# Finer pieces and other places for the weights of an mLSTM cell and a multiplicative FFN on one Trainium2 core

## The chip, the cores and the metric

The kernel runs on one core of a Trainium2 chip. The metric is the device time of one execution in microseconds (us). The core has five engines with a queue each: TensorE (PE, matmuls; its weight loads are listed as PEld), VectorE (DVE), ScalarE (ACT), GpSimd (POOL) and SyncE (SP, which here only issues DMAs). An engine works through its own instructions in order and waits for others by semaphores. Traces are taken by the hardware profiler; times in them are us from the start of the span.

## The reference, cut to what matters

```python
# q, k, v, o_gate: (4, 8, 768, 40); i_gate, f_gate: (4, 8, 768); all float32
for t in range(768):                                   # mLSTM cell
    m_new  = max(f[t] + m, i[t])
    C = exp(f[t] + m - m_new) * C + exp(i[t] - m_new) * outer(v[t], k[t])
    n = exp(f[t] + m - m_new) * n + exp(i[t] - m_new) * k[t]
    y[t] = sigmoid(o_gate[t]) * (C @ q[t]) / max(|n . q[t]|, 1)
    m = m_new
x   = y as (3072, 320)                                 # tokens x (heads * dims)
out = (((x @ w1) * (x @ w2)) @ w3) @ w_out             # w1, w2: 320x1024, w3: 1024x1024, w_out: 1024x320
```

The four weights arrive as 64-bit floats, so that each of their elements is two 32-bit words, and the kernel turns them into 32-bit floats itself.

## The kernel before

**Units and steps.** The cell is computed in chunks. A unit n is 128 tokens of one batch (two chunks of 64, all 8 heads); there are 24 of them (NU), and n = 4c + b. The main loop has 32 steps s. Step s computes unit s's scores (`ss`, k times q) and its contribution to the state (`pc`), and finishes unit s-1: `ph` (scores times v), `pi` (state times q), then on DVE the division, the gate and `y` (L430 to L457). These four live in two PSUM tiles named `cell`. `x_trans` (px) turns y into `xT`, the FFN's input; `turn` (pt) turns k and q of the next unit.

**FFN.** `up` multiplies x by w1 (tile `pa`) and w2 (`pb`) for two blocks of 128 columns (f, f+1) and 256 tokens; `up_rest` adds the last 64 of 320 rows from `wr` (both weights' last rows), ACT copies `pa` to `a_sb` (L647) and DVE multiplies it with `pb` into `ab` (L648). For the first 256 tokens step 2 uses columns 0 to 255, step 3 256 to 511, step 4 512 to 767 and step 5 768 to 1023. w3 and w_out are folded into one matrix `w3o` (`w3_mm`, tile `wp`, from step 10 on), and `ffn_out` multiplies `ab` by it (tile `po`, or `cell`), copies it to `o_sb` on ACT (L750) and sends it out. From step 19 on `up_by_seven` does x times w1 and w2 with seven products in place of eight (tiles `pa`, `pb` and `p`); it reads sums of weights, which `weight_sums` makes on POOL (L668, eight instructions in all), and sums of tokens, which `token_sums` makes on DVE (L675, four instructions for each group of tokens, the first at the end of step 18).

**Weights.** `fetch` issues the DMA of one piece into a buffer of raw words, `scale_next` scales it with two ACT instructions (L196, L200), and `convert` makes 32-bit floats of it with L204 and L205 on DVE (for w_out L205 is on POOL; for w3 a transpose, L253, follows). Raw words lie in a ring of four buffers, or in `idle` ones: memory of `w3o` and `wo` that nothing uses yet. w1, w2 and `wr` come in ten pieces: five for columns 0 to 511 (w1 twice, w2 twice, `wr`), then five for columns 512 to 1023, 512 KB each. `n_cvt` says how many conversions each step has at its end, `n_fetch` how many pieces are fetched by then.

**Order.** Every engine's instructions keep the order in which the code issues them (`in_order` for PE, `keep_order` for the others), and `issue_after` puts some behind a named instruction. PSUM tiles of `mps` come from a ring of four banks, so that a tile waits for the readers of the tile four places before it. `warm` issues dummy matmuls (tile `fill`). In step 2 `between` stands in the middle of the cell's work, in step 3 one conversion (`late`) stands in two places of it. U is a row of exponents for each head; `rows_of_u` (L300, DVE) spreads it for a unit, from unit 10 on it comes back from DRAM (`load_u`), and `weights` (L308, ACT, eight instructions) makes the exponentials of a unit from it, which `masks` (L313, POOL) cuts. `out_gate` (L275, ACT) is the gate's tanh on `o_in`, which `load_o` brings.

The places that the change touches: `warm` L97, `fetch` L216, the `idle` list L529, the tables `w12` and `n_cvt` L821 and L823, the DMAs of a step L834 to L850, `between` L898, the place of `weights` and `out_gate` for s > 15 (NY) L919, the counts L956, and the place of `weight_sums` L974.

```python
n_cvt = [0, 0, 2, 0, 1, 2, 3, 3, 3] + [2] * 6
n_fetch = [5, 5, 10]
...
for n in () if s == 1 else (s + 2,) if s < B else (s + 2, s + 3) if s == B else (s + 3,):
    if n < N_U:
        rows_of_u(n)
...
for _ in range(n_cvt[s] if s < len(n_cvt) else 0):
    convert()
    converted += 1
...
while todo and fetched < (n_fetch[s] if s < len(n_fetch) else converted + 4):
    fetch(*todo.pop(0))
```

Of the kernel before, what the change touches and what calls it, by code (L numbers as in the profile page):

```python
# [16 lines left out]
def kernel(  # L17
# [29 lines left out]
    L = 64  # L47
    P = 128
    NT = S // L
    NT2 = S // P  # L50
    NU = NT2 * B
# [3 lines left out]
    DM = H * D  # L55
# [3 lines left out]
    KF = DM // P  # L59
    REM = DM - KF * P  # L60
# [30 lines left out]
    def mm(out, lhsT, rhs, start=True, stop=True):  # L91
        in_order(nc.tensor.matmul(out, lhsT=lhsT, rhs=rhs, start=start, stop=stop))  # L92
# [1 line left out]
    def transpose(out, in_, n=P):  # L94
        in_order(nc.tensor.transpose(out, in_, ident[0:n, 0:n]))  # L95

    def warm(n, m=4, small=0):  # L97
        bank = mps([P, 4, P], "fill")
        for _ in range(n):
            mm(bank[:, 0:m], ident, ident.unsqueeze(1).to_broadcast([P, m, P]))  # L100
        for i in range(small):
            r = halves[i % 2]
            mm(bank[r, 0, 0:L], ident[r, 0:L], ident[r, 0:L])

    halves = [slice(0, L), slice(L, P)]
    heads = [slice(0, D), slice(DP, DP + D)]
# [11 lines left out]
    ident = const.tile([P, P], FP, name="ident")  # L118
# [7 lines left out]
    NY = 15  # L126
# [9 lines left out]
    def load(n, which=slice(0, 3)):  # L136
        for dst, src in ((kbuf[n % NB][:, :, 0:D], k), (qbuf[n % NBQ][:, :, 0:D], q), (vbuf[n % NBV][:, :, 0:D], v))[which]:
            if src is not q or n < N_DVE:
                nc.sync.dma_start(out=dst, in_=rows(src, n))  # L139
# [16 lines left out]
    def load_o(n):  # L156
        o_t[n] = io.tile([P, H, D], FP, name="o_in", tag="o_in", bufs=5)
        nc.sync.dma_start(out=o_t[n], in_=rows(o_gate, n))  # L158
# [17 lines left out]
    wr = const.tile([2 * REM, DFF], FP, name="wr")  # L176
    w3o = const.tile([128, FO, DM], FP, name="w3o")
    CW = 512
    w1_d, w2_d, w3_d, wo_d = (x.bitcast(U32) for x in (moe_w1, moe_w2, moe_w3, moe_w_out))

    idle = []
# [25 lines left out]
    def cols(c0, n):  # L207
        return slice(2 * c0, 2 * (c0 + n))

    every = slice(0, 128)  # L210
# [5 lines left out]
    def fetch(kind, i, part):  # L216

        if kind == "w12":
            c0 = part * CW
            if i < 2 * KF:  # L220
                wt, src = ((w1, w1_d), (w2, w2_d))[i // KF]
                ko = i % KF
                dst, pieces = wt[:, ko, c0:c0 + CW], [(every, src[ko * 128:(ko + 1) * 128, cols(c0, CW)])]
            else:
                dst, pieces = wr[:, c0:c0 + CW], [(slice(j * REM, (j + 1) * REM), src[KF * P:DM, cols(c0, CW)])
                                                  for j, src in enumerate((w1_d, w2_d))]
        elif kind == "wo":
            dst, pieces = wo[:, i, :], [(every, wo_d.rearrange("(p i) n -> p i n", i=FO)[:, i, :])]
        else:
            dst, pieces = None, [(square, w3_d[i * 128 + part * 64:i * 128 + (part + 1) * 64, cols(j * CQ, CQ)]  # L230
                                  .rearrange("(m r) n -> r m n", m=2)) for j, square in enumerate(squares)]
        pend.append((dst, raw_tile(dst.shape[-1] if dst is not None else CW, pieces), i, part))
# [9 lines left out]
    def convert():  # L242
        if not scaled:
            scale_next()
        dst, raw, ko, half = scaled.pop(0)
        if dst is not None:
            to_f32(dst, raw, nc.gpsimd if dst.shape[-1] == DM else nc.vector)
            return
        w3 = wst.tile([128, CW], FP, name="w3", tag="w3")
        to_f32(w3, raw, nc.vector)  # L250
        if half == 0:
            w3T_t[ko] = wst.tile([128, FO, 128], FP, name="w3T", tag="w3T")
        nc.vector.transpose(out=w3T_t[ko].rearrange("c k (m r) -> c m k r", r=32)[:, 2 * half:2 * half + 2],  # L253
                            in_=w3.rearrange("r (m c k) -> r m k c", m=2, k=FO))
        if half:
            turned_w3.append(ko)
# [17 lines left out]
    def out_gate(n):  # L274
        nc.scalar.activation(out=o_t[n], in_=o_t[n], func=AF.Tanh, scale=0.5)  # L275
# [22 lines left out]
    def rows_of_u(n):  # L298
        c, b = divmod(n, B)
        nc.vector.transpose(out=weights_tile(n).rearrange("p h (t i) -> p h t i", t=2),  # L300
                            in_=UT[:, :, (0, 2, 1)[c], b * H:(b + 1) * H].rearrange("p t h -> p h t").unsqueeze(3).to_broadcast([P, H, 2, 32]))

    def weights(n):
        c, b = divmod(n, B)
        src = weights_tile(n) if n else spread(n)
        pw = weights_tile(n)
        for h in range(H):
            nc.scalar.activation(out=pw[:, h, :], in_=src[:, h, :], func=AF.Exp, bias=aT[:, c, b * H + h:b * H + h + 1])  # L308
# [7 lines left out]
    def turn(n):  # L316


        if n >= N_DVE:
            for src, dst, name in zip(turned_in[n % 2], (kT_t, qT_t), ("kT", "qT")):  # L320
                dst[n] = sb.tile([128, NP, P], FP, name=name, tag=name)
                done = nc.vector.transpose(out=dst[n].rearrange("i p (r f) -> i p f r", f=4),
                                           in_=src[:, 32:TB].rearrange("i (p f d) -> i p f d", p=NP, f=4)[:, :, :, 0:32])
            return done
        for src, dst, name in ((kbuf[n % NB], kT_t, "kT"), (qbuf[n % NBQ], qT_t, "qT")):
            pt = mps([128, NP, P], "pt")
            for p in range(NP):
                transpose(pt[:, p, :], src[:, 2 * p:2 * p + 2, :].rearrange("p a b -> p (a b)"))
            dst[n] = sb.tile([128, NP, P], FP, name=name, tag=name)
            nc.scalar.copy(out=dst[n], in_=pt)  # L330
# [184 lines left out]
    for i, r in enumerate(third):  # L515
# [4 lines left out]
    w3o_words, wo_words = (t.rearrange("p f d -> p (f d)").bitcast(U32).rearrange("p (n two) -> p n two", two=2)  # L520
                           for t in (w3o, wo))
# [4 lines left out]
    load(1)  # L526
    fetch("w12", 2, 0)
    load_o(0)
    idle += [words[:, i * CW:(i + 1) * CW] for words in (w3o_words, wo_words) for i in range(2)]  # L529
    fetch("w12", 3, 0)  # L530
    load_o(1)
    fetch("w12", 4, 0)
# [285 lines left out]
    n_seven = [0] * 19 + [1] * 12 + [0]  # L818
    n_down = [0] * 16 + [2] * 5 + [1] * 4 + [0] * 7
    n_out = [0] * 27 + [1, 0, 1, 0, 3]  # L820
    w12 = [("w12", i, part) for part in range(2) for i in range(2 * KF + 1)]  # L821
    todo = w12[5:] + [("wo", i, 0) for i in range(FO)] + [("w3", ko, part) for ko in range(FO) for part in range(2)]
    n_cvt = [0, 0, 2, 0, 1, 2, 3, 3, 3] + [2] * 6  # L823
    n_fetch = [5, 5, 10]
    pinned, ahead = 32, 9
    behind = ExitStack()
    turned, converted, fetched = 0, 2, 5

    for s in range(len(n_up)):
# [3 lines left out]
            load_u(s + 3)  # L833
        if s < 3:  # L834
            if s == 2:
                for _ in range(3):
                    fetch(*todo.pop(0))
            load(s + 2, slice(0, 2))
            if s == 1:
                load_o(2)  # L840
            if s == 2:
                for _ in range(2):
                    fetch(*todo.pop(0))
                fetched = 10
            load(s + 2, slice(2, 3))
            if s:
                load_o(s + 2)
        elif s + 2 < NU:
            load(s + 2)
            load_o(s + 2)  # L850
        if s < NU:
            if s >= B:
                decayed(state[s % B][1], state[s % B][0], s, 0)
# [16 lines left out]
        if n_seven[s]:  # L870
            seven = up_by_seven(*sevens.pop(0), (lambda i: cell[i // 2][:, i % 2].rearrange("p (i t) -> p i t", i=2)) if s <= NU else
                                lambda i: mps([128, 2, TH], "p67" if i < 2 else "p15"), nc.gpsimd if sevens else nc.vector)
            if s <= NU:
                seven[0]()
            seven[1]()
        if seven and s <= NU:
            ffn_out([downs.pop(0) for _ in range(n_down[s])], [cell[1][:, i, 0:DM] for i in range(2)])
        else:
            for _ in range(n_down[s]):
                ffn_out([downs.pop(0)])  # L880
# [17 lines left out]
        def between():  # L898
            twice(1)
            weighted(2)  # L900
            rows_of_u(3)
            for _ in range(3):
                scale_next()
            for n in range(2):
                x_trans(n)
                if n == 0:
                    warm(1, small=38)
            for _ in range(3):
                convert()
            turn(2)  # L910
            block = up(*now[0])
            weighted(3)
            weights(3)
            masks(3)
            out_gate(2)
            convert()
            up_rest(*block)

        if NY < s < NU:  # L919
            if s < NU - 1:  # L920
                weights(s + 1)
            out_gate(s)
        gated = None
        if s <= NU:
            gated = quarter_work(s, rest, between if s == 2 else None, convert if s == 3 else None)
# [27 lines left out]
            cell_psum.close()  # L953
            banks.extend([ps_m] * 3 + [ctx.enter_context(tc.tile_pool(name="ps_x", bufs=4, space=bass.MemoryType.PSUM))] * 4)
        if s in (2, 3):
            turned, converted = 2, converted + (4 if s == 2 else 2)  # L956
        while turned < min(s - 1, NY):
            x_trans(turned)
            turned += 1
# [2 lines left out]
        if s < NU:  # L962
# [7 lines left out]
                masks(s + 1)  # L970
            if s != 2 and s <= NY:
                out_gate(s)
        if s in (16, 17):
            weight_sums(s - 16)  # L974
        if s == B:
            nc.gpsimd.memset(gates[RG:P, 0:5 * TC], 0.0)
            for i, r in enumerate(third):
# [46 lines left out]
```

## Time and profile before

| what | value |
|---|---|
| median of three runs | 427.96 us (427.51 to 430.15) |
| the profiled execution, its own time | 427.13 us |
| its span in the trace | 425.4 us |
| DVE busy | 299.0 us (70%) |
| ACT busy | 182.9 us (43%) |
| POOL busy | 166.6 us (39%) |
| DMA's mean rate over the span | 109 GB/s |

The span is the time from the first to the last instruction; the rest of the execution's time lies around it. The profile has a page with busy shares, the chain of work that ended last and the costliest groups of instructions. The trace behind it gives timelines: a line is the start, the duration, the engine, the line of code, the operation, what it writes and reads and its shape; xN says that N such instructions are put together; brackets hold the idle time of the engine just before, and what ended it. A table by stretches gives each engine's busy time in a stretch, then the granted clock of PE (1.00 is full speed), the DMA engines' busy share and GB/s.

### The profile page before, as it was taken

The page shows a single profiled execution, that of the slowest core. Times are in us where ns is not written, and L with a number is a line of the kernel's source. Part 1 is how long each engine was busy: PE and PEld are TensorE (multiplying, and loading weights), DVE is VectorE, ACT ScalarE, POOL GpSimd, SP SyncE. Part 2 cuts the span into 40 slices and gives each one's busy share as a digit, 9 for nine tenths or more (in the row PEclk, how much of TensorE's full clock was granted, in tenths as well). Part 3 has the DMA queues.
Part 4 walks back from the last instruction along what each step waited for, and adds up shares of the span by engine and source line. Part 5 has one row for each costly group of instructions (what it writes and reads, how often), then busy time and mean ns, then how long its engine had stood idle before and what let it go on. Part 6 is the DMA issues. An engine that isn't in the chain of part 4 may idle for free.

```text
span 425.4 us, 13074 instructions
## 1 busy us (share of the span) xinstructions
PE 413.4 (97%) x5353; PEld 335.1 (79%) x5353; DVE 299.0 (70%) x561; ACT 182.9 (43%) x516; POOL 166.6 (39%) x219
## 2 busy tenths in 40 slices
PE   7999899999999999999999899999999999999997
PEld 3778788887788778878777678688778879888896
DVE  6767977688847857867445846396867599575972
ACT  4776866567543745752555416054432210210000
POOL 4530473442302312312327742557453587542100
PEclk9999999999999999999999899999999999999999
DMA  8989986889884484951508771724211110000001
GB/s 188 227 164 247 213 144 128 186 200 209 177 154 118 100 177 132 158 101 40 112 31 160 149 137 57 139 74 90 55 42 38 29 39 2 32 2 31 2 32 62
DMA packets 124555, 46.56 MB, mean 109 GB/s; under 512 B 104720, under 2 KB 116304, under 8 KB 124496
## 3 DMA queue, kind: packets, MB, share of 16 engines
q1 hardware_dynamic: 120896, 41.70, 48.0%
q10 hardware_dynamic: 3600, 4.03, 2.7%
q8 instruction: 42, 0.69, 0.7%
q14 instruction: 17, 0.14, 0.1%
HBM read 39.91 MB, written 5.80 MB: 107 GB/s over the span
## 4 chain that ended last, share of the span: by engine, by line
PE 83%; SPq 6%; DVE 4%; DMA 3%; issue 2%; ACT 1%; POOL 0%; DVEq 0%; ACTq 0%; POOLq 0%
PE cell L92 21%; PE pa L92 20%; PE pb L92 13%; PE wp L92 8%; PE o L92 8%; PE po L92 6%; SPq L139 3%; PE p L92 3%; SPq L189 2%; DMA raw<-in_moe_w_dram 1%; PE px L95 1%; DMA wo<-in_moe_w_dram 1%; DVE pw L779 1%; PE pt L95 1%; SPq L158 1%
## 5 line engine op out<-in xcount | busy, mean ns | idle before, releaser
L340 POOL TENSOR_TENSOR state<-state,decay 128x164 f32<-128x164 f32 x40 | 23.4, 586 | 143.2 <-DVE state L409 115.9
L92 PE MATMUL pa<-xT,w 128*128 128x256 f32 x240 | 60.8, 384 | 0.0
L92 PEld LDWEIGHTS pa<-xT,w 128*128 128x128 f32 x240 | 44.7, 191 | 6.5
L308 ACT ACTIVATE pw<-pw,aT 128x64 f32<-128x64 f32 x184 | 46.4, 337 | 3.3 <-ACT o_sb L750 2.7
L92 PE MATMUL pb<-xT,w 128*128 128x256 f32 x192 | 45.6, 380 | 0.7 <-DVE w L205 0.7
L738 POOL TENSOR_TENSOR ab<-ab,a_sb 128x512 f32<-128x512 f32 x22 | 29.4, 1358 | 31.7 <-DVE ab L693 31.7
L92 PEld LDWEIGHTS pb<-xT,w 128*128 128x128 f32 x192 | 36.4, 190 | 6.0 <-DVE w L205 1.1
L720 POOL TENSOR_TENSOR wo<-wo 128x512 f32<-128x512 f32 x22 | 27.4, 1269 | 28.4 <-DVE wo L695 28.4
L92 PE MATMUL pa<-xT,wr 64*64 64x256 f32 x384 | 37.0, 386 | 0.6 <-DVE wr L205 0.6
L92 PE MATMUL wp<-wo,w3T 128*128 128x320 f32 x128 | 35.9, 433 | 1.4 <-issue 0.8
L92 PE MATMUL pb<-xT,wr 64*64 64x256 f32 x384 | 36.4, 380 | 0.0
L313 POOL TENSOR_SCALAR_AFFINE_SELECT pw<-pw 64x512 f32<-64x512 f32 x48 | 33.1, 690 | 7.9 <-ACT pw L308 6.4
L647 ACT ACTIVATE a_sb<-pa 128x512 f32<-128x512 f32 x24 | 14.3, 596 | 49.9 <-PE pb L92 49.9
L648 DVE TENSOR_TENSOR ab<-pb,a_sb 128x512 f32<-128x512 f32 x24 | 16.4, 687 | 27.5 <-ACT a_sb L647 27.4
L92 PE MATMUL cell<-w3o,ab 128*128 128x320 f32 x128 | 35.5, 433 | 0.0
L92 PEld LDWEIGHTS wp<-wo,w3T 128*128 128x128 f32 x128 | 23.8, 190 | 10.8 <-issue 1.0
L92 PEld LDWEIGHTS cell<-w3o,ab 128*128 128x128 f32 x128 | 24.2, 190 | 9.6 <-ACT wo L711 0.2
L92 PEld LDWEIGHTS pa<-xT,wr 64*64 64x64 f32 x384 | 18.9, 132 | 15.5 <-issue 8.8
L695 DVE SCALAR_TENSOR_TENSOR a_sb<-pa,wo 128x512 f32<-128x512 f32 x12 | 8.3, 689 | 32.5 <-PE pa L92 32.5
L92 PE MATMUL po<-w3o,ab 128*128 128x320 f32 x96 | 26.4, 433 | 0.0
L92 PEld LDWEIGHTS po<-w3o,ab 128*128 128x128 f32 x96 | 18.1, 190 | 7.3
L437 ACT COPY h<-cell 64x164 f32<-64x164 f32 x56 | 16.2, 290 | 16.8 <-DVE y L430 16.3
(185 smaller groups left out, 886.0 us busy)
## 6 DMA issues: line engine op xcount, KB each, us to landing
raw<-in_moe_w_dram SPq DMA_DIRECT2D x64, 128.0 KB, 3.3
kbuf<-in_k_dram SPq DMA_DIRECT2D x24, 160.0 KB, 4.4
v_all<-in_v_dram SPq DMA_DIRECT2D x24, 160.0 KB, 4.6
o_in<-in_o_gate_dram SPq DMA_DIRECT2D x24, 160.0 KB, 4.8
pw<-U_d SPq DMA_DIRECT2D x28, 128.0 KB, 3.5
raw<-in_moe_w_dram SPq DMA_DIRECT2D x5, 512.0 KB, 5.7
raw<-in_moe_w_out_dram SPq DMA_DIRECT2D x8, 320.0 KB, 4.0
out_dram<-o_sb ACTq DMA_DIRECT2D x14, 160.0 KB, 2.0
```

The lines of the kernel that those rows point to most:

```text
L92: in_order(nc.tensor.matmul(out, lhsT=lhsT, rhs=rhs, start=start, stop=stop))
L95: in_order(nc.tensor.transpose(out, in_, ident[0:n, 0:n]))
L139: nc.sync.dma_start(out=dst, in_=rows(src, n))
L189: nc.sync.dma_start(out=dst, in_=src)
L308: nc.scalar.activation(out=pw[:, h, :], in_=src[:, h, :], func=AF.Exp, bias=aT[:, c, b * H + h:b * H + h + 1])
L313: nc.gpsimd.affine_select(out=pw[r], in_=pw[r], compare_op=OP.is_ge, fill=0.0, base=0, pattern=[[0, H], [1, L]], channel_multiplier=-1)
L340: nc.gpsimd.tensor_tensor(out=new, in0=old, op=OP.mult, in1=decay[:, b * NP:(b + 1) * NP, 2 * c + x:2 * c + x + 1] .to_broadcast([P, NP, D1]))
L437: nc.scalar.copy(out=h[halves[x], 0:H // 2] if x == e else h[halves[x], H // 2:H], in_=ph[x][halves[e]])
L647: nc.scalar.mul(out=a_sb, in_=pa, mul=UP ** -2)
L648: nc.vector.tensor_tensor(out=ab_t[gr][j][:, fs[0]:fs[-1] + 1, t0:t0 + a_sb.shape[-1]], in0=pb, in1=a_sb, op=OP.mult)
L720: aside_by.tensor_tensor(out=kept[j][:, 1:4:2], in0=kept[j][:, 1:3], in1=kept[j][:, 3:4].to_broadcast([128, 2, TH]), op=OP.add)
L738: aside_by.tensor_tensor(out=t[:, f:FO:FH, :], in0=t[:, f:FO:FH, :], in1=a, op=OP.mult)
```

## The change

- The second five pieces of w1, w2 and `wr` become ten: five for columns 512 to 767, then five for 768 to 1023, 256 KB each. The first five quarters go to `idle` memory of `wo`, the others to that of `w3o`. The first are fetched in step 2 (all five ahead of k and q of unit 4), the others in step 3.
- The first five quarters are converted at the end of step 2 (three) and in step 3 (two), the others at the end of step 4 (five). The table of conversions for steps 5 to 8 goes from 2, 3, 3, 3 to 2, 3, 3, 4. (Step 4 converted one piece of w_out before.) w_out and w3 are fetched later accordingly.
- The gate o of a unit is loaded a step later, by SP.
- In step 2 the conversions stand ahead of `rows_of_u(3)`, there are three instead of four, and the fill is two 128x512 matmuls instead of one and 38 of 64x64.
- For steps 16 to 23, the exponentials of the next unit and the gate's tanh are issued ahead of `ffn_out`, so ahead of the copies to `o_sb` on ACT.
- `weight_sums` runs at the end of steps 15 and 16 instead of 16 and 17.

```diff
-    def warm(n, m=4, small=0):
+    def warm(n, m=4):
...
-            c0 = part * CW
+            c0, n = ((0, CW), (CW, CW // 2), (CW + CW // 2, CW // 2))[part]
...
-                dst, pieces = wt[:, ko, c0:c0 + CW], [(every, src[ko * 128:(ko + 1) * 128, cols(c0, CW)])]
+                dst, pieces = wt[:, ko, c0:c0 + n], [(every, src[ko * 128:(ko + 1) * 128, cols(c0, n)])]
...
-    idle += [words[:, i * CW:(i + 1) * CW] for words in (w3o_words, wo_words) for i in range(2)]
+    idle += [w3o_words[:, i * CW:(i + 1) * CW] for i in range(2)]
+    idle += [words[:, i * CW // 2:(i + 1) * CW // 2] for words, order in ((wo_words, range(5)), (w3o_words, (4, 0, 1, 2, 3)))
+             for i in order]
...
-    w12 = [("w12", i, part) for part in range(2) for i in range(2 * KF + 1)]
+    w12 = [("w12", i, part) for part in range(3) for i in range(2 * KF + 1)]
...
-    n_cvt = [0, 0, 2, 0, 1, 2, 3, 3, 3] + [2] * 6
+    n_cvt = [0, 0, 3, 0, 5, 2, 3, 3, 4] + [2] * 6
...
             if s == 2:
-                for _ in range(3):
+                for _ in range(5):
                     fetch(*todo.pop(0))
             load(s + 2, slice(0, 2))
             if s == 1:
                 load_o(2)
             if s == 2:
-                for _ in range(2):
-                    fetch(*todo.pop(0))
+                load_o(3)
                 fetched = 10
             load(s + 2, slice(2, 3))
-            if s:
-                load_o(s + 2)
         elif s + 2 < NU:
-            load(s + 2)
-            load_o(s + 2)
+            load(s + 2, slice(0, 2))
+            if s == 3:
+                for _ in range(5):
+                    fetch(*todo.pop(0))
+                fetched = 15
+            load(s + 2, slice(2, 3))
+            load_o(s + 1)
+        elif s + 2 == NU:
+            load_o(s + 1)
...
+        if NY < s < NU:
+            if s < NU - 1:
+                weights(s + 1)
+            out_gate(s)
         if seven and s <= NU:
             ffn_out([downs.pop(0) for _ in range(n_down[s])], [cell[1][:, i, 0:DM] for i in range(2)])
...
             weighted(2)
-            rows_of_u(3)
             for _ in range(3):
                 scale_next()
             for n in range(2):
                 x_trans(n)
                 if n == 0:
-                    warm(1, small=38)
+                    warm(2)
             for _ in range(3):
                 convert()
+            rows_of_u(3)
             turn(2)
             block = up(*now[0])
...
             out_gate(2)
-            convert()
             up_rest(*block)
 
-        if NY < s < NU:
-            if s < NU - 1:
-                weights(s + 1)
-            out_gate(s)
...
-            turned, converted = 2, converted + (4 if s == 2 else 2)
+            turned, converted = 2, converted + (3 if s == 2 else 2)
...
-        if s in (16, 17):
-            weight_sums(s - 16)
+        if s in (NY, NY + 1):
+            weight_sums(s - NY)
```

More of the change, by code (lines that the diff above doesn't have):

```diff
@@ L100, in warm @@
             mm(bank[:, 0:m], ident, ident.unsqueeze(1).to_broadcast([P, m, P]))
-        for i in range(small):
-            r = halves[i % 2]
-            mm(bank[r, 0, 0:L], ident[r, 0:L], ident[r, 0:L])
     halves = [slice(0, L), slice(L, P)]
@@ L222, in fetch @@
                 ko = i % KF
-                dst, pieces = wt[:, ko, c0:c0 + CW], [(every, src[ko * 128:(ko + 1) * 128, cols(c0, CW)])]
+                dst, pieces = wt[:, ko, c0:c0 + n], [(every, src[ko * 128:(ko + 1) * 128, cols(c0, n)])]
             else:
-                dst, pieces = wr[:, c0:c0 + CW], [(slice(j * REM, (j + 1) * REM), src[KF * P:DM, cols(c0, CW)])
+                dst, pieces = wr[:, c0:c0 + n], [(slice(j * REM, (j + 1) * REM), src[KF * P:DM, cols(c0, n)])
                                                   for j, src in enumerate((w1_d, w2_d))]
```

## The prediction

> **What bounds the kernel now.** I read the busy shares first, then the chain of waits, then TensorE's timeline for every idle stretch, then the timelines of the engines named there. The page says that TensorE (PE) is the bound:
>
> ```profile
> span 425.4 us, 13074 instructions
> ...
> PE 413.4 (97%) x5353; PEld 335.1 (79%) x5353; DVE 299.0 (70%) x561; ACT 182.9 (43%) x516; POOL 166.6 (39%) x219
> ```
>
> PE is idle for 12 us in all (425.4-413.4), 4.3 of them before 25 us (by the table by stretches). So the change is worth what it does to PE's idle stretches, and to PE's clock. PE's timeline of the head shows three places that the diff touches: a fill of dummy matmuls at 22.47, and two waits in step 4, whose 0.66 and 0.55 in brackets are idle time with its releaser:
>
> ```profile
> 22.47 3.38 PE L92 MATMUL fill<-ident 128*128 128x512 f32 x78
> 25.78 0.55 PE L95 MATMUL px<-ident,y 128*128 128x128 f32 x3
> ...
> 43.55 1.56 PE L92 MATMUL pb<-xT,w 128*128 128x256 f32 x6 [0.66 <-DVE w L205]
> 45.66 0.43 PE L92 MATMUL pa<-xT,wr 64*64 64x256 f32 x1 [0.55 <-DVE wr L205]
> ...
> 49.64 1.89 PE L92 MATMUL pa<-xT,w 128*128 128x256 f32 x8
> ```
>
> The last line is step 5's `up`. It reads the last quarter of w1 and does not wait, since all halves were converted in step 3. VectorE (DVE) at that moment is far behind PE: it closes step 4 only here (two rows of U, then the step's one conversion, of w_out):
>
> ```profile
> 52.98 1.29 DVE L300 STREAM_TRANSPOSE pw<-UT 128x512 f32<-128x512 f32 x2
> 54.20 0.66 DVE L204 TENSOR_SCALAR wo<-raw 128x320 uint32<-128x320 uint32 x1
> ```
>
> Two later waits. At step 10 PE waits 0.64 us for a PSUM bank that DVE's product L648 frees, and L648 stands behind step 8's conversions of w3:
>
> ```profile
> 104.81 5.38 PE L92 MATMUL wp<-wo,w3T 128*128 128x320 f32 x19 [0.64 <-DVE ab L648]
> ```
>
> ```profile
> 101.81 0.39 DVE L204 TENSOR_SCALAR w<-raw 128x512 uint32<-128x512 uint32 x1
> 102.33 0.69 DVE L205 CUSTOM_DVE_ANT_0 w<-raw,w 128x1024 uint16<-128x1024 uint16 x1
> 103.06 1.12 DVE L253 STREAM_TRANSPOSE w3T<-w 128x512 f32<-128x512 f32 x1
> 104.11 1.24 DVE L648 TENSOR_TENSOR ab<-pb,a_sb 128x512 f32<-128x512 f32 x2
> ```
>
> At step 19 PE waits for the token sums L675, three of which take 1.38 to 1.49 us where the first takes 0.43; from 235.97 on POOL runs its weight sums L668 beside them. The table by stretches (PE busy first, granted clock in the column before DMA's share) shows that this wait also halves the clock:
>
> ```profile
> 240.52 1.22 PE L92 MATMUL pa<-w3T,w 128*128 128x256 f32 x2 [1.43 <-DVE w3T L675]
> ```
>
> ```profile
> 239.00:240.00 1.00, 0.10 (x1) 0.00 (x0) 1.00 (x2) 0.86 (x4) 1.00 (x1) 1.00 1.06 222
> 240.00:241.00 1.00, 0.48 (x1) 0.48 (x2) 1.00 (x3) 0.09 (x1) 0.79 (x2) 0.75 1.03 217
> 241.00:242.00 1.00, 1.00 (x4) 0.73 (x4) 0.47 (x1) 0.96 (x4) 0.00 (x0) 0.50 0.58 96
> ```
>
> The clock is 0.50 or 0.54 until 244. Four matmuls start at 240.52 and the fifth at 244.01: 3.49 us where four take 1.73 (a `pa` x8 line of the chain). So a halved clock costs 1.76 us, once.
>
> **The change part by part.** The sum goes against the profiled execution, 427.13 us (span 425.4), which lies 0.83 below the median of the runs (427.96).
>
> Fill, and conversions ahead of rows of U (step 2). Two 128x512 fills take about 2 us (one took 1.02 to 1.13) in place of 3.38. The second `px` needs POOL's copy of y, done at 24.23, so it starts at about 24.4, not 25.78. Its ACT copy waits for the one before (24.75+0.47), so xT is there at 25.7 and `pa` starts at about 25.75 in place of 27.04: 1.3 us. The three conversions start 0.63 us sooner, so w2 is ready well before `pb`. Rows of U, moved behind them, end near 28.7 in place of 24.5; ScalarE's (ACT) exponentials started at 27.76 and are put off by 1 us; `a_sb`, next on ACT, goes to 31.2, and its reader on DVE was idle until 33.13. Free.
>
> Quarters (steps 2 to 4). Ten pieces of 256 columns in place of five of 512: the same bytes, five more instruction pairs on each of ACT and DVE. The w pieces that step 4 reads are 1.25 MB in place of 2.5, and o's 160 KB no longer lies ahead of them on SP's queue. Before, ACT took the third 512 KB piece at 36.11 and the fifth at 42.63; 1.25 MB is between the second and the third, so all is in by about 35. DVE's fourth and fifth conversion then end where DVE's own order puts them: in the trace 3.84 and 5.96 behind the start of step 3's `ab` (39.65 to 43.49 and 45.61), with quarters about 3.4 and 5.0. That `ab` follows step 3's `up` (37.83, less 1.3) by 0.7, so they end near 40.6 and 42.2; PE needs them at 41.4 and 42.7. Both waits go: 43.55-42.73 and 45.66-44.85, 1.63 us. With the 1.3 step 4's `up` ends at 43.65 in place of 46.58. The slack is under 1 us, so the gain lies between 1.3 and 3.2.
>
> What is late next: the other five pieces. They are converted at the end of step 4 (n_cvt[4] is 5), behind L300 x2 on DVE, and step 5's `pa` reads the first. In the trace, from the end of step 4's `up` (46.58) to `pa` of step 5 (49.64) are 3.06 us; L430 to the place of the conversions (48.32 to 54.20) are 5.88, and L430 itself starts at least 1.3 after `up` ends (`a_sb` 0.6, `ab` 0.6). So PE arrives at 43.65+3.06 = 46.7, DVE at 43.65+1.3+5.88 = 50.8, and the first piece is ready one conversion later. A 512-column pair takes 1.13 (37.35 to 38.48); a quarter lies between 0.57 and 1.13, I take 0.65 as L204 and L205 do not shrink to half, and 0.2 for POOL's masks, beside which step 8's first conversion was longer by 0.5. Ready at 51.6: PE idles 4.9 us (3.9 to 6). ACT is no later: its scaling pairs come to 0.65 by the 320- and 512-column rows (pitch 0.385 and 0.56). An idle of 1.43 halved the clock, so this one does: `pa` 3.49, `pb` 1.73, rest 0.91, end 57.7, where it was 54.10. The head's balance is **+3.6** (between +1.5 and +5).
>
> w_out and w3 later (n_cvt, n_fetch). Twelve conversions from step 5 to step 8 as before by step 8, but step 7 has three w_out and step 8 four w3, not three. One w3 conversion is 2.30 us of DVE (101.81 to 104.11). DVE has no slack there: step 8's `y` hangs on PE, L648 is already 2.3 late. L648 moves to 106.4, `wp` to 107.1: +2.30, and PE's idle there becomes 2.94. Does that halve the clock? Idles of 0.64 and 0.75 (at 141) did not, 1.43 did; 2.94 lies beyond, so I add 1.7. **+4.0** (0 if DVE catches up, 2.3 without the clock). [...]
>
> Weight sums a step sooner. POOL idles 11.8 us ahead of 220.67, so the first four (1.3 each) fit into step 15 and the other four take the first four's place (223.7 to 228.7). Then L675 runs alone, 4x0.43 from 235.8, ends at 237.6, and PE needs it at 238.83. The wait (240.52-238.83 = 1.69) and the half clock (1.76) go: **-3.45** (0 to -3.5). Next in line is DVE's L419, which frees the bank of step 19's second pair of shared products: L430 to L419's end took 4.0 (240.39 to 244.40), L430 can start at 237.7, so 241.7 against a need at 246.2-3.45 = 242.7.
>
> Exponentials and o's tanh ahead of `o_sb` (steps 16 on), o a step later on SP: PE has no other wait there until 355.8, and DVE's h (1.74 idle for ACT at 217 and 228) comes sooner. o is issued one step ahead, 12 us against a landing of 4.8. Cost 0; if that cover were gone, tanh would hold `y`, at up to 1 us a step.
>
> Sum: 427.13 + 3.6 + 4.0 - 3.45 = 431.3. The median was 0.83 above the profiled run; I put half of that on top and predict **431.7**.
>
> **The rivals.**
> 1. Conversions arrive in time, as the change's words suggest: DVE, no longer held up by late halves, closes step 4 before PE needs w1. For it: DVE sat idle 4.52 us at 33 for a DMA. Against: the chain from step 4's `up` to the conversions starts with PE's own output, so earlier work does not shorten it. Without that wait and with step 10's: 427.13-2.9+4.0-3.45 = 424.8; without either 420.8.
> 2. The clock stays up after step 10's wait: 429.6.
> 3. Slower by more than 1%: the last five pieces land late. They are issued on SP behind k, q, v and o, into w3o's space. It decides from the point where a piece lands after ACT's turn for it, near 50; at 240 KB/us (512 KB per 2.15 us, 32.43 to 34.58) the 3.46 MB issued from 26.8 on (two sets of pieces, six loads) should be in near 41, 8 us of cover. Each us later costs a us: 2 late give 433.7.
> 4. The late wait stays, because POOL's sums meet DVE's transposes in step 15 and 16: 434.7 at most.
>
> **How the numbers follow.** Forecast 0.47 (own range 430.5 to 433.5); rival 1 0.16; rival 2 0.17; rival 3 0.13; rival 4 0.07. The measurement of this kernel tells about 1% (4.3 us) from no change, so faster means below 423.7 and slower above 432.2. Rival 1 straddles 423.7 and gives most of faster, 0.12. Slower: rivals 3 and 4, and the upper third of the forecast: 0.36. Same: 0.52. The range of 424.5 to 434.5 leaves out the better half of rival 1 and the end of rivals 3 and 4.
>
> **What would show it.** Right: a PE wait of 4 to 6 us at about 46 to 52 put down to DVE w L205, with the clock near 0.5 behind it; no waits in step 4; a wait near 3 us ahead of `wp` at step 10; L675 at 0.43 and no clock below 1 near 240. Wrong: PE without idle between 46 and 60, or `wp` with 0.6 us of wait; then the kernel is faster by what these would have cost.

## The result, and the profile after

| | before | after |
|---|---|---|
| median of 20 runs each | 427.11 us (426.0 to 432.26) | 430.19 us (427.61 to 434.23) |
| ratio after / before, with its 95% interval | | 1.0067 [1.0045, 1.009] |
| profiled execution, its span | 427.13 us, 425.4 us | 434.23 us, 432.5 us |

The change costs 3.1 us, 0.7%. The profiled execution of after is the slowest of its runs, 4 us above their median, and that of `after_again` below is the slowest of its eight, so their traces are read for places, and for sums only beside the experiments.

The page after, its span, its busy shares and the row of the granted clock over 40 slices of 10.8 us:

```profile
span 432.5 us, 12964 instructions
...
PE 416.5 (96%) x5279; PEld 336.8 (78%) x5279; DVE 297.3 (69%) x571; ACT 183.8 (42%) x526; POOL 164.9 (38%) x219
...
PEclk9869969999999999999999999999999999999999
```

PE has 16.0 us idle in place of 12.0, and is itself busy for 3.1 us longer with 37 fewer matmuls (74 in the count, which has each of these twice). So the loss is idle time and clock together. The clock row names the places: slices 2, 3 (about 11 to 32 us) and 6 (54 to 65). Behind these it is full (1.00 in each stretch of 5 us of the table from 65 us on), at 240 us too.

PE's timeline of after from 18 to 63 us, the lines that answer to those of the head before (start, duration, ..., idle before it and what ended it):

```profile
18.75 1.00 PE L92 MATMUL cell<-qT,kT 40*64 40x64 f32 x25 [1.24 <-issue]
...
25.76 3.22 PE L92 MATMUL fill<-ident 128*128 128x512 f32 x4
...
30.02 1.89 PE L92 MATMUL pa<-xT,w 128*128 128x256 f32 x8
...
43.55 1.89 PE L92 MATMUL pa<-xT,w 128*128 128x256 f32 x8
45.28 1.89 PE L92 MATMUL pb<-xT,w 128*128 128x256 f32 x8
...
56.77 4.21 PE L92 MATMUL pa<-xT,w 128*128 128x256 f32 x8 [5.53 <-DVE w L202]
60.77 2.79 PE L92 MATMUL pb<-xT,w 128*128 128x256 f32 x8
```

Four things are to be seen. Step 4 (43.55) has no wait any more. Step 5's `pa` waits 5.53 us for the first conversion of the last quarter, the new wait that was forecast. Its eight matmuls take 4.21 us where they took 1.89. And a gap that was not forecast stands at 18.75, in the middle of the cell's small matmuls: its releaser is "issue", so the profile shows no other engine that ended it.

DVE's timeline of after at that wait (L201 and L202 are L204 and L205 of before) shows what the conversion stands behind:

```profile
53.53 0.77 DVE L454 SCALAR_TENSOR_TENSOR y<-o_in,h 128x320 f32<-128x320 f32 x1
54.22 1.29 DVE L297 STREAM_TRANSPOSE pw<-UT 128x512 f32<-128x512 f32 x2
55.44 0.62 DVE L201 TENSOR_SCALAR w<-w3o 128x256 uint32<-128x256 uint32 x1
56.20 0.43 DVE L202 CUSTOM_DVE_ANT_0 w<-w3o,w 128x512 uint16<-128x512 uint16 x1
```

The conversion waits for its turn, behind step 4's division, gate and two rows of U. ACT is hardly earlier: in its order the scaling of the piece stands behind a unit's exponentials and the gate's tanh, and ends at 54.88, 0.56 us before DVE's turn. ACT's timeline of after:

```profile
54.14 0.43 ACT L193 ACTIVATE w3o<-w3o 128x256 f32<-128x256 f32 x1
54.46 0.42 ACT L197 ACTIVATE w3o<-w3o 128x256 uint32<-128x256 uint32 x1
```

The table by stretches of after (length, PE, PEld, DVE, ACT, POOL busy, granted clock, DMA's share, GB/s) shows the clock at both places:

```profile
20.00:21.00 1.00, 1.00 (x19) 0.76 (x9) 0.48 (x1) 1.00 (x5) 0.00 (x0) 0.50 0.61 89
...
55.00:56.00 1.00, 0.00 (x0) 0.00 (x0) 1.00 (x2) 1.00 (x4) 0.88 (x3) 0.88 1.06 361
56.00:57.00 1.00, 0.23 (x1) 0.26 (x2) 0.86 (x3) 1.00 (x4) 1.00 (x1) 0.50 0.93 305
61.00:62.00 1.00, 1.00 (x3) 0.79 (x3) 0.00 (x0) 0.00 (x0) 0.00 (x0) 0.50 0.30 37
62.00:63.00 1.00, 1.00 (x5) 0.81 (x4) 0.00 (x0) 0.00 (x0) 0.00 (x0) 0.71 0.00 0
```

The clock drops while PE still waits (the mean of 0.88 in 55 to 56) and comes back between 62 and 63, 5.2 to 6.2 us after PE has resumed at 56.77. By the mean granted clock it does so in every execution: that mean is 0.992 or less in all 28 of after and `after_again`, and the half clock from 56 to 62 by itself makes a mean of about 0.992 (an estimate: in the rows from 55 to 63 the clock falls short by 3.4 of 432 us).

At step 10 PE's timeline of after has no wait ahead of the first `wp` at all:

```profile
113.66 0.55 PE L95 MATMUL px<-ident,y 128*128 128x128 f32 x3
114.04 6.36 PE L92 MATMUL wp<-wo,w3T 128*128 128x320 f32 x23
```

although DVE is as late there as was forecast. Its timeline of after:

```profile
115.44 1.11 DVE L250 STREAM_TRANSPOSE w3T<-w 128x512 f32<-128x512 f32 x1
116.46 1.25 DVE L647 TENSOR_TENSOR ab<-pb,a_sb 128x512 f32<-128x512 f32 x2
```

The product L647, L648 before, begins 2.4 us after `wp` has begun. Before, `wp` waited for it.

At step 19 POOL's sums are over (POOL has no busy time from 245 to 250), the sums of tokens run alone, and PE does not wait. DVE's timeline of after:

```profile
245.24 0.42 DVE L674 TENSOR_TENSOR w3T<-xT,w3T 128x256 f32<-128x256 f32 x1
245.58 0.42 DVE L674 TENSOR_TENSOR w3T<-xT 128x256 f32<-128x256 f32 x1
245.92 0.42 DVE L674 TENSOR_TENSOR w3T<-xT,w3T 128x256 f32<-128x256 f32 x1
```

Three of these took 1.38 to 1.49 us before, beside POOL's sums.

### The profile page after: what moved, and what is told of

Read it like the earlier page. It is cut to its first block, busy times and chain, and to the rows that moved or that the text cites. A ratio compares the mean times of both kernels' runs of the same rounds, so it can differ in the third digit from the quotient of the medians.

```text
span 432.5 us, 12964 instructions
## 1 busy us (share of the span) xinstructions
PE 416.5 (96%) x5279; PEld 336.8 (78%) x5279; DVE 297.3 (69%) x571; ACT 183.8 (42%) x526; POOL 164.9 (38%) x219
## 4 chain that ended last, share of the span: by engine, by line
PE 90%; DVE 5%; issue 2%; ACT 2%; DMA 0%; POOL 0%; SPq 0%; DVEq 0%; ACTq 0%; POOLq 0%
PE cell L92 23%; PE pa L92 22%; PE pb L92 14%; PE wp L92 8%; PE o L92 8%; PE po L92 6%; PE p L92 3%; PE px L95 2%; PE pt L95 2%; PE fill L92 1%; DVE pw L778 1%; PE ph L92 1%; DVE ab L692 1%; DMA gates<-in_f_gate_dram 0%; ACT pw L305 0%
## 5 line engine op out<-in xcount | busy, mean ns | idle before, releaser
L92 PE MATMUL pa<-xT,w 128*128 128x256 f32 x240 | 62.6, 392 | 5.6 <-DVE w L202 5.5
L92 PEld LDWEIGHTS pb<-xT,w 128*128 128x128 f32 x192 | 37.3, 194 | 5.3
L647 DVE TENSOR_TENSOR ab<-pb,a_sb 128x512 f32<-128x512 f32 x24 | 16.4, 688 | 34.9 <-ACT a_sb L646 34.8
```

The costliest lines, as they stand in the source:

```text
L647: nc.vector.tensor_tensor(out=ab_t[gr][j][:, fs[0]:fs[-1] + 1, t0:t0 + a_sb.shape[-1]], in0=pb, in1=a_sb, op=OP.mult)
```

## The experiments

My theory after the result: the loss is step 5's wait with its clock, less the gain of the late parts; step 10's forecast failed because `wp` no longer takes the bank that the late product frees; the head's shorter fill gives nothing at the median. Rivals: that the step-5 conversions only move DVE's lateness about and cannot be had for less; that step 10's wait went for another reason (DVE caught up); that the weight sums bring the full 3.45 us. Each ratio is to the kernel before, timed beside it on the same chip, in three groups: `after_again` to `early_in_step4` (median of before 426.16 us), `before_again` to `late_parts` (426.91) and `early_old_fill` (426.28). The ratio is not that of the medians, and can differ from it by some tenths of a per cent.

**after_again**: the changed kernel itself, beside the next three.

> The changed kernel once more, for a trace without the head's disturbance (an issue gap of 1.24 us at 18 us and a halved clock behind it in the first trace). Theory (step 5's wait is the loss): against before 1.007 (1.003 to 1.011); the PE wait put down to DVE w L202 at step 5 is 4.5 to 6 us, the clock is 0.50 for 4 to 6 us behind it, no wait ahead of the first wp, none near step 19. Rival (the head's gap of 18 us belongs to the change): the gap of over 1 us near 18 is there again and the clock halves in the head.

429.21 us, 1.0085 [1.0049, 1.0122]. PE's timeline has both marks of the result again:

```profile
19.98 0.62 PE L92 MATMUL cell<-qT,kT 40*64 40x64 f32 x25 [1.05 <-issue]
...
56.15 4.21 PE L92 MATMUL pa<-xT,w 128*128 128x256 f32 x8 [5.63 <-DVE w L202]
```

So neither is a matter of one execution alone, and again no wait stands ahead of the first `wp` or near step 19. From this `pa` to step 6's `pa` are 10.78 us (66.93-56.15), where before has 7.77 (57.41-49.64): 3.0 us lost behind the wait.

**sums_alone**: the kernel before with nothing but the earlier sums of weights.

```diff
-        if s in (16, 17):
-            weight_sums(s - 16)
+        if s in (NY, NY + 1):
+            weight_sums(s - NY)
```

> The kernel before with the weight sums alone moved to steps 15 and 16. Theory: the wait for the token sums (1.69) and the halved clock behind it (1.76) both go, so 3.4 us less: ratio 0.992 (0.990 to 0.994), L675 at 0.42 to 0.48 us each, granted clock 1.00 near 240. Rival (only the wait goes, the clock falls anyhow): 1.7 us less, 0.996. Rival (POOL's sums in step 15 delay masks or states): no gain, 1.000.

424.61 us, 0.9978 [0.9952, 1.0005]: 1.55 us less by the medians, and the interval takes in no gain at all. DVE's timeline has the mechanism (line L675, numbers of before):

```profile
235.74 0.43 DVE L675 TENSOR_TENSOR w3T<-xT,w3T 128x256 f32<-128x256 f32 x1
236.08 0.42 DVE L675 TENSOR_TENSOR w3T<-xT 128x256 f32<-128x256 f32 x1
236.42 0.42 DVE L675 TENSOR_TENSOR w3T<-xT,w3T 128x256 f32<-128x256 f32 x1
```

The wait is gone and the clock is 1.00 throughout 235 to 240. Half of the 3.45 forecast is missing; `before_again` bears on where.

**ring_of_banks**: the changed kernel with its four PSUM banks as four pools of one bank, taken strictly in turn. No other work changes.

```diff
-    ps_m = ctx.enter_context(tc.tile_pool(name="ps_m", bufs=4, space=bass.MemoryType.PSUM))
+    ps_m = [ctx.enter_context(tc.tile_pool(name=f"ps_m{i}", bufs=1, space=bass.MemoryType.PSUM)) for i in range(4)]
...
-    banks = [ps_m]
+    banks = list(ps_m)
```

> The changed kernel with four PSUM pools of one bank each, used strictly in turn, instead of one pool of four banks whose next bank is chosen at build time. Theory (the predicted wait of step 10 failed to come only because the first wp got the bank that ACT frees, not the one that DVE's product frees): the wait comes back, 2.5 to 3.2 us ahead of the first wp put down to DVE ab L647, clock halved behind it, 3 to 4.7 us more than the changed kernel: ratio to before about 1.016 (1.012 to 1.020). Rival (the four conversions would not have been late anyhow): no wait there, 1.007.

435.85 us, 1.0232 [1.0192, 1.0273]; the changed kernel beside it has 429.21. PE's timeline at step 10:

```profile
111.50 0.55 PE L95 MATMUL px<-ident,y 128*128 128x128 f32 x3
115.00 7.34 PE L92 MATMUL wp<-wo,w3T 128*128 128x320 f32 x20 [2.96 <-DVE ab L647]
```

and the table by stretches:

```profile
115.00:116.00 1.00, 1.00 (x3) 0.73 (x4) 0.97 (x3) 1.00 (x3) 0.00 (x0) 0.73 0.85 193
116.00:117.00 1.00, 1.00 (x4) 0.61 (x3) 0.97 (x3) 1.00 (x3) 0.00 (x0) 0.50 0.58 195
...
118.00:119.00 1.00, 1.00 (x4) 0.68 (x3) 0.84 (x4) 0.73 (x2) 0.48 (x1) 0.57 0.75 191
119.00:120.00 1.00, 1.00 (x5) 0.71 (x4) 0.80 (x2) 0.51 (x1) 0.86 (x2) 1.00 0.83 181
```

This is the forecast wait, nearly to the hundredth (2.94), with the half clock behind it. So DVE had not caught up: what spares the changed kernel the wait is the bank. The programs as built say the same. In their lists of instructions the first two tiles `wp` have these banks and wait for these engines:

```
before  wp_1912 (bank 2)  waits DVE                    wp_1922 (bank 0)  waits Activation
after   wp_1896 (bank 0)  waits DVE and Activation     wp_1906 (bank 2)  waits DVE
ring    wp_1905 (bank 2)  waits DVE                    wp_1915 (bank 3)  waits Activation
```

In after the first `wp` takes bank 0, which ACT's copy `a_sb` frees early (the last copy ahead of it ends at 112.67), and its wait on DVE is for `w3T`; the bank that DVE's product frees goes to the second `wp`, and that starts late enough: the two products end at 117.71, and it starts at about 118.4 (an estimate, 114.04 and half of the 8.78 us that the 32 records of both tiles take). The 6.6 us between the two medians is more than this wait and clock (about 4.7: 2.96, and 1.7 by the mean clock of 0.66 from 115 to 120). By the traces the rest lies ahead of step 6: its `pa` starts at 65.33 in the ring, and at 60.83 in `filled_wait` below, or 63.0 with the 2.2 us of clock which that run saves. The ring alters banks there too; which of them costs these 2.3 us is open.

**early_in_step4**: the changed kernel with the five conversions in step 4 moved from its end to right behind `up_rest`, ahead of the division. `convert` issues the scaling too, so ACT's part moves with DVE's, ahead of the exponentials and the tanh.

```diff
-    n_cvt = [0, 0, 3, 0, 5, 2, 3, 3, 4] + [2] * 6
+    n_cvt = [0, 0, 3, 0, 0, 2, 3, 3, 4] + [2] * 6
...
+            if s == 4:
+                for _ in range(5):
+                    convert()
...
+        if s == 4:
+            converted += 5
```

> The changed kernel with the last five conversions put right behind the product of step 4 on DVE (and their scaling behind a_sb on ACT), ahead of h, in place of the end of step 4. Theory: the wait of step 5 (5.5 us) and the halved clock behind it (about 3) go, as w1's last quarter is ready 2.1 us behind that product's end at most; 7 to 9 us less than the changed kernel: ratio to before 0.988 (0.984 to 0.993). Rival A (the pieces have not landed yet when ACT's turn comes): PE waits for DVE w L202 all the same, with ACT waiting for DMA w3o; 1.000 to 1.005. Rival B (the chain of y, put off by 3.9 us, becomes the wait): PE waits at ph or px of the next step, 0.995 to 1.000.

422.98 us, 0.9927 [0.9898, 0.9956]: by the medians 3.2 us less than before and 6.2 less than the changed kernel. PE's timeline has step 5 without the wait, and a small one where the delayed work is read:

```profile
17.86 0.62 PE L92 MATMUL cell<-qT,kT 40*64 40x64 f32 x25 [0.41 <-issue]
...
48.25 2.24 PE L92 MATMUL pa<-xT,w 128*128 128x256 f32 x8
...
53.82 0.68 PE L92 MATMUL cell<-v_all,pw 64*64 64x41 f32 x32 [0.58 <-DVE pw L399]
```

DVE's timeline shows the order that does it: the conversions stand behind the product and ahead of L427.

```profile
46.21 0.65 DVE L647 TENSOR_TENSOR ab<-pb,a_sb 128x512 f32<-128x512 f32 x1
46.79 0.64 DVE L201 TENSOR_SCALAR w<-w3o 128x256 uint32<-128x256 uint32 x1
...
50.74 0.42 DVE L202 CUSTOM_DVE_ANT_0 wr<-w3o,wr 128x512 uint16<-128x512 uint16 x1
51.09 0.49 DVE L427 TENSOR_TENSOR h<-cell,gT 128x328 f32<-128x328 f32 x1
```

The quarters were there by 46.8, so it was their place in the orders of ACT and DVE that cost the 6.2 us, and no transfer. This run does not part the two engines; by after's rows, with DVE's work moved alone the scaling would have held the conversion back to 54.88. Nor is the place free: from this `pa` to step 6's are 9.53 us (57.78-48.25) where before has 7.77, so 1.8 us are still lost, and the wait with what follows it cost some 8.0.

**before_again**: the kernel before, unchanged, for a second look at its wait at step 19.

> The kernel before once more, for a second trace. The weight sums alone gained about 1.6 us by the medians, not the 3.4 by which the two traces differ. Theory (whether the clock halves behind the wait of step 19 differs from execution to execution): the wait for the token sums is 1.4 again; the clock near 240 may be 1.00 throughout. Rival (the clock halves every time): 0.50 near 240 again. Also: a PE gap put down to issue near 18 us, as in three of four traces with the changed head, or none.

428.93 us, span 427.2. PE's timeline and the table by stretches:

```profile
243.91 0.70 PE L92 MATMUL pa<-w3T,w 128*128 128x256 f32 x2 [1.41 <-DVE w3T L675]
```

```profile
243.00:244.00 1.00, 0.09 (x1) 0.09 (x1) 1.00 (x2) 0.26 (x1) 1.00 (x2) 1.00 1.01 188
244.00:245.00 1.00, 1.00 (x5) 0.90 (x6) 0.87 (x2) 0.68 (x3) 0.18 (x1) 1.00 0.46 73
```

The same wait, and the clock stays at 1.00. So the half clock behind 1.4 us of idle, which I had priced at 1.76 us in every execution, comes in some and not in others. The mean granted clock of each execution says how often at most: 1.76 us lost of 427 makes 0.996, the profiled execution of before has 0.995, and 49 of the 67 beside the experiments have 0.999 or 1.00. With the clock in 18 of 67 the earlier sums are worth 1.9 to 2.2 us (an estimate: 1.43 to 1.69 for the wait, 0.47 for the clock), which is the lower edge of the interval of `sums_alone` and inside that of `late_parts` below. So the clock is the likely part of what is missing, but no run shows it by itself.

**head_alone**: the kernel before with the fill and the order of step 2 of the change; sizes of pieces as before.

```diff
-            rows_of_u(3)
...
-                    warm(1, small=38)
+                    warm(2)
             for _ in range(3):
                 convert()
+            rows_of_u(3)
```

> The kernel before with the change of step 2 alone: two 128x512 fills instead of one and 38 small ones, rows of U behind the three conversions. Theory: the second px 1.3 us sooner, nothing behind it later: 0.997 (0.994 to 0.999). Rival (the changed head's issue gap near 18 us and the halved clock behind it come with these instructions): the gap is there, the clock is 0.50 behind it, and the ratio is 1.000 to 1.008.

427.77 us, 1.0032 [1.0010, 1.0053]: a loss of 1.4 us by the ratio (0.9 by the medians) in place of the forecast gain of 1.3. PE's timeline, of the slowest of the twelve executions:

```profile
17.82 0.82 PE L92 MATMUL cell<-qT,kT 40*64 40x64 f32 x25 [0.57 <-issue]
...
43.27 1.01 PE L95 MATMUL pt<-ident,q_all 128*128 128x128 f32 x4 [2.92 <-issue]
```

The gap near 18 us is there with this part alone. A second, of 2.92 us, stands at 43.27, where neither before nor after has one, with a lowered clock behind it (0.70 in the mean from 40 to 45 and 0.62 from 45 to 50; over the execution 0.987). The clock does not explain the missing gain: five of the twelve have a mean clock of 1.00, and their median, 427.28, is still above before's 426.91. A rival is that step 4's waits swallow it: all four traces of before's sizes and old fill have them (1.2 to 3.3 us in sum between 39 and 48), and what comes there sooner may only wait longer. No run tests that.

**filled_wait**: the changed kernel with six dummy matmuls (the x12 `fill` of the trace) in front of step 5's `up`, so that PE is busy while it waits. They are extra work.

```diff
         now = [ups.pop(0) for _ in range(n_up[s])]
+        if s == 5:
+            warm(6)
```

> The changed kernel with six dummy 128x512 matmuls (5.2 us) on TensorE ahead of step 5's up, where it waits for the last quarter of w1. Theory (the wait costs twice, 5.6 us of idle and a halved clock behind it worth about 3): the idle turns into dummy work, the clock stays 1.00, pa of step 5 takes 2.4 us at most (it is paced by the conversions), and 2 to 3.5 us go: ratio to before 1.001 (0.997 to 1.005). Rival (pa is slow because the conversions pace it): nothing goes, 1.008.

427.74 us, 1.0037 [1.0013, 1.0061], against 1.0085 for the change without it: some 2 us. PE's timeline:

```profile
23.73 0.56 PE L95 MATMUL px<-ident,y 128*128 128x128 f32 x3
...
25.53 1.89 PE L92 MATMUL pa<-xT,w 128*128 128x256 f32 x8
...
46.65 5.32 PE L92 MATMUL fill<-ident 128*128 128x512 f32 x12
52.25 0.70 PE L92 MATMUL pa<-xT,w 128*128 128x256 f32 x2 [0.28 <-DVE w L202]
53.62 1.56 PE L92 MATMUL pa<-xT,w 128*128 128x256 f32 x6 [0.67 <-DVE w L202]
```

The clock stays at 1.00 and from this `pa` to that of step 6 are 8.58 us, not 10.78. So 2.2 of the 3.0 us behind the wait were the clock; the other 0.8 is the pace of DVE's conversions (0.67 of it in the bracket). In this execution the gap near 18 us is absent, and the head goes as forecast: `pa` of step 2 starts at 25.53 (25.75 forecast), and PE reaches step 5 at 46.65 (46.7 forecast).

**late_parts**: the kernel before with the earlier sums, and with the exponentials and the gate's tanh ahead of `ffn_out`.

```diff
+        if NY < s < NU:
+            if s < NU - 1:
+                weights(s + 1)
+            out_gate(s)
         if seven and s <= NU:
...
-        if NY < s < NU:
-            if s < NU - 1:
-                weights(s + 1)
-            out_gate(s)
...
-        if s in (16, 17):
-            weight_sums(s - 16)
+        if s in (NY, NY + 1):
+            weight_sums(s - NY)
```

> The kernel before with the two late changes alone: the weight sums a step sooner, and from step 16 on exponentials and tanh ahead of the copies to o_sb. Theory (the exponentials' place costs and gains nothing): as with the sums alone, 0.998 (0.994 to 1.000). Rival (the copies to o_sb, put off by 2.4 us, hold PSUM banks or the cell's tile): PE waits behind ffn_out from step 16 on, 1.000 or more.

424.93 us, 0.9952 [0.9931, 0.9972]: 2.0 us less. Against `sums_alone` the intervals overlap, so the exponentials' place costs nothing that can be measured, and whether it gains is open.

**early_old_fill**: `early_in_step4` with the fill of before.

```diff
-                    warm(2)
+                    warm(1, small=38)
```

> The kernel with step 4's early conversions, and the fill of the kernel before (one 128x512 and 38 small matmuls) in place of two large ones. Theory (the changed fill, with 37 matmuls fewer, moves the places where TensorE waits for its own instructions: near 18 us in four of six traces with it, in none of four without; there the clock halves, which costs more than the 1.3 us that the shorter fill saves): no issue gap near 18, clock 1.00 in the head, the fill 3.4 us again, issue gaps in wp near 141 instead of 165 and 211; ratio to before 0.988 (0.985 to 0.992), under the 0.993 of the kernel with the short fill. Rival (the gaps fall by chance): 0.993 to 0.996, the fill's 1.3 us lost.

423.72 us, 0.9945 [0.9923, 0.9967]; span 421.8, as that of `early_in_step4`. The gap near 18 us is gone, but one of its kind stands at `wp` in PE's timeline, as was expected:

```profile
140.69 4.30 PE L92 MATMUL wp<-wo,w3T 128*128 128x320 f32 x15 [1.08 <-issue]
```

So the gap near 18 goes with the shorter fill, and the old fill is not faster for being without it: the gain expected here did not come. The gap at `wp` goes with the old fill: all five traces with it have one there (0.36 to 1.08 us), and none of the six with the shorter fill has.

## Why the prediction was right in the sum, and where it was wrong

431.7 us were predicted and 430.19 measured, within 1% of before as the likeliest case had it. But the largest term did not come, and two others were off by about 1.5 us each the other way. The place and the cause of the loss were foreseen; that the sum came so near is in part luck.

| term (as predicted) | predicted, us | shown, us |
|---|---|---|
| balance of the head, to step 6 | +3.6 (1.5 to 5) | about +5.1, by the difference below |
| step 10: wait 2.30 and clock 1.7 | +4.0 | 0 |
| late parts: sums of weights, order on ACT | -3.45 | -2.0 (`late_parts`) |
| sum | +4.15 | +3.1 (430.19-427.11) |

The head's 5.1 is what is left, 3.1+2.0; it was not measured by itself, and it comes from two groups of runs. The trace of `filled_wait`, whose head is undisturbed, agrees: step 6's `pa` is 3.4 us behind that of before (60.83-57.41), and the clock which that run saves is 2.2, so 5.6 in all.

- **Step 4's waits: right.** Both are gone, from each trace with the quarters.
- **Step 5's wait: right in place, cause and size; mis-sized in its clock.** 4.9 us of idle were predicted from DVE's order, 5.53 and 5.63 measured. Behind it 1.76 were put for the clock; 3.0 were lost, 2.2 of them to the clock and 0.8 to the pace of the conversions (`filled_wait`), which the prediction left out. These are 0.6, 0.4 and 0.8 us more than predicted, about what the head's balance is over. That ACT is no later was right by 0.56 us only. By `early_in_step4` the wait and what follows it cost 6.2 us more than an early place in the order.
- **Fill and conversions ahead of U: failed at the median.** The step was "it starts at about 24.4 ... 1.3 us". Where PE is undisturbed it holds (`filled_wait`: second `px` at 23.73, `pa` at 25.53). But four of the six traces with the shorter fill have a gap of 0.41 to 1.24 us near 18 us, ended by "issue", and in after the clock is 0.50 behind it, so `pa` of step 2 starts at 30.02 instead of 27.04. None of the five traces with the old fill has such a gap, though in both traces of before the 28 matmuls at this place take 1.07 us where 27 of them in `sums_alone` take 0.62. That the 37 matmuls less move the places of these gaps fits this, and was not shown. At the median the half clock near 18 is absent: 13 of the 20 executions of after have a mean clock of 0.991 or 0.992, which step 5's alone makes. What the shorter fill is worth there is open: `head_alone` says a loss, `early_old_fill` against `early_in_step4` does not.
- **Step 10: failed.** The step was "L648 moves to 106.4, `wp` to 107.1". The product was late as predicted, but `wp` did not need its bank. I had taken the four banks for a strict ring, "the tile four places before", on the strength of the wait in before. The allocator assigns the banks when the program is built, and the change altered the assignment. `ring_of_banks` shows that under the assumed ring the step would have been right. The prediction's own sign of being wrong, a `wp` with little wait, came true; the kernel was not 4 us faster for it than forecast because the head and the weight sums took most of that back.
- **Sums of weights: mechanism right, mis-sized.** The wait went and L675 fell to 0.42, as said. But the clock's 1.76 was taken from one execution; `before_again` has the wait without it, and at most 18 of 67 executions of before can have had it.
- **Exponentials, tanh and o: right.** No wait of PE came, and `late_parts` is not slower.

On how long an idle has to be to halve the clock, the runs give no rule. The prediction went by one row, 1.43 us with a halved clock behind it, and took longer idles to do the same. The long ones did: 5.5 us in after and 2.96 in `ring_of_banks`. The wait of 1.4 at step 19 did in one of its three traces (1.43 in before, but neither 1.41 in `before_again` nor 1.41 in `head_alone`). What decides it for the short one, no run shows.

## What to carry to other kernels

When a transfer is split, look at the place of the conversion in the order of each engine that has a part in it: here the same five conversions cost 6.2 us more at the end of a step than behind the product, where they left waits of under 0.6 us. Before adding up a wait for a buffer, read in the changed program which buffer each tile got, and do not infer a ring from one wait. A clock loss seen behind a short idle in one trace may be a chance and not a constant: here it came in at most 18 of 67 executions, so look at the mean clock of the others before it goes into a sum at its full price.

## What the runs showed of the hardware

- A halved clock outlasted the wait: 5.2 to 6.2 us after PE resumed in after; in the ring, from the stretch 115 to 116 into that of 118 to 119. Behind the wait of 5.5 us it came in all 28 executions (mean clock 0.992 or less), behind that of 1.4 us in at most 18 of 67. With dummy matmuls in the long wait the mean clock was 0.995 or more in all twelve.
- PE stopped for 0.2 to 2.9 us with "issue" as the only releaser. The places differed between programs: at `wp` near 141 to 145 us with the old fill, near 155 to 167 and again 201 to 214 in five of the six traces with the shorter one, and in four of these near 18 as well. The length differed between executions of one program: 0.75 and 1.03 us at the same `wp` in the two of before, of which the second alone has one at 59.02 (1.48).
- A sum of two SBUF operands on DVE took 0.41 to 0.43 us alone at step 19 (after, `sums_alone`) and 1.38 to 1.50 us beside POOL's sums (before, `before_again`).
